# Two narrow recurrences taken chunk by chunk in turn instead of one after the other, with feed-forward blocks of 64 positions of four batches

## The chip, the cores and the metric

The kernel runs on one core of one Trainium2 chip. The metric is the device time of one execution in microseconds (us); lower is better. PE is TensorE, DVE is VectorE, ACT is ScalarE, POOL is GpSimd, SP is SyncE, which issues all DMAs here.

## The reference

Three stages follow each other. The first is a recurrence over 768 positions in 4 batches and 8 heads, with a state of 40 x 40 for each of these 32 pairs. The second and third are feed-forward layers (320 to 2048 to 320) over the 3072 tokens that the first stage gives, each with another activation.

```
for t in range(S):                                   # S = 768
    y[:, :, t] = einsum('bhd,bhde->bhe', rt, state)
    Sa = einsum('bhde,bhe->bhd', state, at)
    state = state * wt[:, :, None, :] - einsum('bhd,bhe->bhde', Sa, bt) + einsum('bhd,bhe->bhde', vt, kt)
x = y.transpose(0, 2, 1, 3).reshape(B * S, H * D)    # 3072 x 320
h = x @ w_in;   x = (h * tanh(softplus(h))) @ w_out      # layer 1 (Mish)
h = x @ w_in2;  out = (h * cos(h)) @ w_out2              # layer 2
```

The feed-forward weights arrive as 64-bit floats and are converted on the chip.

## The kernel before

**The recurrence.** Positions are taken in chunks of 32. Inside a chunk the recurrence is a small triangular system, solved by an inverse and a few matrix products; from chunk to chunk the state is handed on. A "half" (`hf`) is two of the four batches with all heads, 16 units; there are two halves of 24 chunks, 48 chunks `g` in all. Before, all chunks of half 0 come first (`hf, c = divmod(g, NCH)`), then those of half 1. So there is one chain of 48 steps.

**Work of one chunk.** `pre(g)` prepares it: a load, two scans on DVE (L548, L554), products (L562, L568), a PE group (L584) evicted in four pieces on DVE (L594), transpositions (L617). It is done up to `LA` = 8 chunks ahead. `inverse_two(bt)` inverts the triangular blocks of a batch of chunks (mostly two): out to HBM and back in another layout (L653), 28 small DVE steps (L663, L665) and a memset (L672), out and back again (L677, L681) into `TT`. `halves` finishes it chunk by chunk: a transposition on DVE (L705), PE (L700), DVE (L708), PE (L702), a copy. `chain(g)` is the serial part: PE groups L760, L773, L805, L829, L853 (two), L896 (two), with evictions on ACT and DVE between them (L765, L379, L837, L864 into `SV` for the next chunk, L872 into `Y`).

**The feed-forward layers.** They work on blocks of 256 tokens in tiles of 256 hidden features. L954 makes `h` of a tile (16 groups of matmuls), layer 1 applies Mish twice on ACT (L1026, L1028) and subtracts on DVE (L1031), so that the value goes on as a high and a low part (`GH`, `GL`); L935 multiplies with `w_out`. A block of layer 1 is four chunks: 128 positions of two batches. Layer 2 uses DVE, Sin on ACT (L1107) and POOL; its last blocks are twice as wide (L969, L985).

**The weights.** `prep` converts each layer's weights in 22 pieces of 128 x 512: a load, a copy of the upper words on ACT (L445), three integer steps on DVE (L449, L454, L459; the third puts the sign in), a rounded copy (L379 into `wih`, `wix`, `woh`) and a subtraction (L486). Layer 1's pieces are done in the first part of the kernel; layer 2's start when the recurrence is over, because they take its memory. The last five pieces of a layer go through one buffer.

**The order.** A planner (`Plan.run`) works out, from durations, hop times and priorities written in the code, in which order each engine's instructions stand. The built program keeps that order. PE is filled with feed-forward work where the recurrence has nothing ready. The planner counts a cost when PE goes from the full array to a part of it or back (`LEAVE`, `CHANGE`, `ENTER`), and time for a new activation table only where a task names its table (`aset`); the tasks of `prep` name none.

## Time and profile before

| | |
|---|---|
| runs | 1143.7 us median of 3 (1140.62 to 1145.07) |
| the profiled execution | 1147.24 us, its span 1145.5 us |
| mean granted TensorE clock | 0.983 of full speed |
| busy share | PE 91%, DVE 71%, ACT 49%, POOL 20% |

The share of an engine is a mean over three stages with different limits: the first 250 us, in which feed-forward work is scarce; the time up to about 650 us, in which recurrence and layer 1 share PE; and the rest, which is feed-forward work alone.

### The profile page before, as it was taken

What the parts mean: (1) busy time and instruction counts of PE and PEld (TensorE: products, weight loads), DVE (VectorE), ACT (ScalarE), POOL (GpSimd) and SP (SyncE); (2) the same over time, 40 slices, a digit from 0 to 9 for tenths busy, and PEclk for the clock granted to TensorE, in tenths of its full rate; (3) what the DMA queues carried; (4) which work ended last, traced back from release to release, by engine and by line L of the source; (5) the groups of instructions that cost most, each with busy time, mean ns of one, the idle gap of its engine ahead of it and who ended that gap; (6) DMA issues with size and microseconds to landing.
All of it is one profiled execution on the core that took longest, in us unless ns stands there. A gap on an engine that the chain in (4) does not pass through costs nothing.

```text
span 1145.5 us, 36557 instructions
## 1 busy us (share of the span) xinstructions
PE 1036.7 (91%) x14888; PEld 941.8 (82%) x14888; DVE 811.2 (71%) x2294; ACT 559.4 (49%) x1382; POOL 225.7 (20%) x276
## 2 busy tenths in 40 slices
PE   1345888989999899999999999999999999999998
PEld 1345677878888788888888999999999999999997
DVE  8989897868898888878973398434655555555554
ACT  3255545545656455555655476444433434343433
POOL 4124110000000000000000033111333333333333
PEclk9999989979999999989999999999999999999999
DMA  7464745445545545445443455221100101010000
GB/s 211 124 171 120 204 100 136 116 129 133 144 137 138 158 123 154 121 127 148 114 116 95 135 156 172 63 63 34 46 26 1 37 15 37 15 31 7 16 8 24
DMA packets 104183, 111.89 MB, mean 98 GB/s; under 512 B 63440, under 2 KB 84176, under 8 KB 104016
## 3 DMA queue, kind: packets, MB, share of 16 engines
q1 hardware_dynamic: 104016, 109.56, 34.6%
q8 instruction: 117, 1.92, 0.7%
q14 instruction: 50, 0.41, 0.1%
HBM read 91.43 MB, written 18.09 MB: 96 GB/s over the span
## 4 chain that ended last, share of the span: by engine, by line
PE 50%; DVE 6%; issue 2%; DMA 2%; ACT 1%; SPq 0%; POOL 0%; DVEq 0%; ACTq 0%; POOLq 0%
PE bank L969 12%; PE bank L985 11%; PE bank L954 11%; PE bank L935 11%; DMA TT<-t_d 1%; DVE SV L864 1%; PE bank L853 1%; PE bank L829 1%; PE bank L1076 1%; DVE GL L1031 1%; PE bank L805 1%; PE bank L773 1%; PE bank L760 1%; DVE FR L837 1%; DVE AM L594 1%
## 5 line engine op out<-in xcount | busy, mean ns | idle before, releaser
L1117 POOL TENSOR_TENSOR GL<-H,GH 128x512 fp32r<-128x512 f32 x96 | 123.8, 1298 | 249.6 <-ACT GH L1115 222.2
L1100 DVE TENSOR_SCALAR T<-bank 128x512 f32<-128x512 f32 x96 | 66.1, 689 | 124.1 <-PE bank L969 111.2
L379 ACT ACTIVATE FL<-bank 64x160 f32<-64x160 f32 (+1 forms) x376 | 101.7, 295 | 103.2 <-PE bank L896 54.7
L1107 ACT ACTIVATE T<-T,half_pi 128x512 f32<-128x512 f32 x96 | 69.0, 719 | 126.1 <-DVE T L1104 126.1
L1031 DVE TENSOR_TENSOR GL<-H,GH 128x512 fp32r<-128x512 f32 x96 | 68.1, 710 | 64.7 <-ACT GH L1028 64.5
L575 POOL MEMSET AM<- 64x256 f32 x96 | 29.5, 308 | 384.3 <-issue 294.3
L954 PE MATMUL bank<-XH,wih 128*128 128x256 f32 x448 | 95.4, 295 | 1.2 <-ACT GH L1028 1.1
L1026 ACT ACTIVATE H<-bank 128x512 f32<-128x512 f32 x96 | 57.3, 597 | 75.6 <-PE bank L954 73.3
L954 PE MATMUL bank<-XL,wih 128*128 128x256 f32 x448 | 90.0, 283 | 0.0
L954 PE MATMUL bank<-XH,wil 128*128 128x256 f32 x448 | 89.8, 282 | 0.0
L1115 ACT ACTIVATE GH<-H 128x512 fp32r<-128x512 f32 x96 | 60.7, 632 | 50.6 <-DVE H L1109 37.6
L853 PE MATMUL bank<-FR,FL 104*64 104x72 f32 x1536 | 67.4, 243 | 13.1 <-DVE FR L837 5.1
L1109 DVE TENSOR_TENSOR H<-bank,T 128x512 f32<-128x512 f32 x96 | 65.7, 685 | 18.0 <-ACT T L1107 17.8
L853 PEld LDWEIGHTS bank<-FR,FL 104*64 104x64 f32 x1536 | 58.8, 148 | 20.0 <-issue 8.7
L954 PEld LDWEIGHTS bank<-XH,wih 128*128 128x128 f32 x448 | 70.4, 193 | 3.2 <-ACT GH L1028 1.3
L584 PE MATMUL bank<-AM,KB 104*64 104x64 f32 x768 | 36.2, 245 | 40.3 <-DVE KB L568 18.5
L665 DVE TENSOR_TENSOR XT<-XM 64x50 f32<-64x50 f32 (+9 forms) x322 | 63.1, 197 | 10.4 <-DMA XM<-l_d 6.5
L954 PEld LDWEIGHTS bank<-XL,wih 128*128 128x128 f32 x448 | 70.0, 193 | 0.0
L954 PEld LDWEIGHTS bank<-XH,wil 128*128 128x128 f32 x448 | 69.9, 193 | 0.0
L954 PE MATMUL bank<-XH,wix 128*128 128x256 f32 x224 | 68.6, 306 | 0.0
L663 DVE TENSOR_TENSOR XM<-XM,XT 64x50 f32<-64x50 f32 (+9 forms) x322 | 64.4, 201 | 4.2 <-DVE XT L665 0.2
L1104 DVE SCALAR_TENSOR_TENSOR T<-T,bank 128x512 f32<-128x512 f32 x96 | 65.5, 682 | 1.6
(174 smaller groups left out, 2976.2 us busy)
## 6 DMA issues: line engine op xcount, KB each, us to landing
IN<-in_inT_dram SPq DMA_DIRECT2D x96, 161.4 KB
VR<-in_vR_dram SPq DMA_DIRECT2D x96, 160.0 KB
FR<-in_rI_dram SPq DMA_DIRECT2D x48, 180.0 KB
FR<-in_vF_dram SPq DMA_DIRECT2D x48, 144.0 KB
TMP<-in_w_in_dram SPq DMA_DIRECT2D x12, 512.0 KB
RA<-in_w_in_dram SPq DMA_DIRECT2D x12, 512.0 KB
RA<-in_w_out_dram SPq DMA_DIRECT2D x10, 512.0 KB
SV<-in_vS_dram SPq DMA_DIRECT2D x96, 52.0 KB
```

Of the source, the lines that this page charges most:

```text
L379: A.activation(o, i, AF.Copy)
L853: PE.matmul(fp[64 * p:64 * p + 64, qp], fl()[0:104, n * D:n * D + 64], fr()[:, n], start=True, stop=True)
L935: PE.matmul(o, l[:, f, tsl], r, start=(first and f == 0 and i == 0), stop=(last and f == 1 and i == 2))
L954: PE.matmul(hp[:, f], pss[i][0], pss[i][1], start=(i == 0), stop=(i == 7))
L969: PE.matmul(bank[P.at((key, "h"))][:, 0:512], pss[i][0], pss[i][1], start=(i == 0), stop=(i == 7))
L985: PE.matmul(o, l, r, start=(ft == 0 and i == 0), stop=(ft == NFF - 1 and i == 2))
L1031: gl = P.add(GLE, (dve(512),), lambda eng, f=f, Hv=Hv, key=key: EN[eng].tensor_tensor(out=GL_t[P.at((key, "gl"))], in0=Hv(f), in1=GH_t[P.a ...
L1100: a = P.add("DVE", dve(512), lambda f=f, hv=hv, Tv=Tv: V.tensor_scalar(out=Tv(f), in0=hv(), scalar1=0.25, scalar2=MAGIC, op0=ALU.add, op1= ...
L1104: b = P.add("DVE", dve(512), lambda f=f, hv=hv, Tv=Tv: V.scalar_tensor_tensor(out=Tv(f), in0=Tv(f), scalar=MAGIC, in1=hv(), op0=ALU.subtra ...
L1107: c = P.add("ACT", act(512, False, 1), lambda f=f, Tv=Tv: A.activation(Tv(f), Tv(f), AF.Sin, scale=-TWO_PI, bias=half_pi), preds=[b], aset ...
L1109: gt = P.add("DVE", dve(512), lambda f=f, Tv=Tv, Hv=Hv, hv=hv: V.tensor_tensor(out=Hv(f), in0=hv(), in1=Tv(f), op=ALU.mult), preds=[c, g_f ...
L1117: gl = P.add("POOL", pool(512), lambda f=f, Hv=Hv, key=key: G.tensor_tensor(out=GL_t[P.at((key, "gl"))], in0=Hv(f), in1=GH_t[P.at((key, "g ...
```

## The change

Chunk numbers now alternate between the halves (`c, hf = divmod(g, 2)`): two chains of 24 steps that need nothing of each other. The state goes to chunk `nx = g + 2`. A block of layer 1 is now 64 positions of four batches, still four chunks. Buffers of the chain (`SV`, `FR`, `VR`, `Y`) are doubled, `LA` falls from 8 to 7, every inverse batch has two chunks, one of each half, and `halves` is done once for both. The planner gets `mate`: a PE task waits a while for the same task of the other half. In `prep` the sign now comes from ACT (`AF.Prelu` with a huge negative slope in place of `AF.Copy`), and the third DVE step is gone. Buffers of the feed-forward layers are cut in halves (`H`, `T`), layer 1's last pieces of `w_out` are done in 128 x 256, and the planner's numbers are changed.

```diff
-NB = 3
+NB = 2
+NEGATIVE = -(2.0 ** 32)
-PULL, PULL_INV, PULL_CH = 0.0, 0, 0
+PULL, PULL_INV, PULL_CH = 0.3, -5000.0, -1e6
-LEAVE, CHANGE, ENTER = 0.14, 0.1, 0.09
+LEAVE, CHANGE, ENTER = 0.22, 0.12, 0.13
+WAIT = 8.0
...
+                        elif t.mate and last_mode == "full" and st - t.ready[e] < WAIT and t.mate.end is None and (
+                                t.mate.n_wait or t.mate.ready[e] > st):
+                            rank = 1.5
...
-    LA = 8
-    N_IN, N_SV, N_FR, N_X, N_VR = 2, 1, 1, 2, 1
+    LA = 7
+    N_IN, N_SV, N_FR, N_X, N_VR, N_Y, N_TT = 2, 2, 2, 2, 2, 2, 3
...
-    BATCH = [(0, 1), (1, 3)] + [(i, 2) for i in range(4, TOT, 2)]
+    BATCH = [(i, 2) for i in range(0, TOT, 2)]
...
-            t1 = P.add("ACT", act(512, False),
-                       lambda raw=raw, av=av: A.activation(av(), raw()[:, :, 1].bitcast(F32), AF.Copy, scale=REBIAS),
+            t1 = P.add("ACT", act(n, False),
+                       lambda raw=raw, av=av: A.activation(
+                           av(), raw()[:, :, 1].bitcast(F32), AF.Prelu, scale=REBIAS, alpha=NEGATIVE),
                        preds=[t0], acq=[(aring, (key, "a"))], prio=prio)
...
-            def cvt3(raw=raw, av=av, uv=uv):
-                u = uv().bitcast(U32)
-                V.scalar_tensor_tensor(out=u, in0=raw()[:, :, 1], scalar=0x80000000, in1=u,
-                                       op0=ALU.bitwise_and, op1=ALU.bitwise_or)
-
-            t3 = P.add("DVE", dve(512, 0.5), cvt1, preds=[t1], prio=prio, port=True)
-            t3 = P.add("DVE", dve(512), cvt2, preds=[t3], prio=prio, port=True)
-            t3 = P.add("DVE", dve(512), cvt3, preds=[t3], rel=[(key, "r")], prio=prio, port=True)
+            t3 = P.add("DVE", dve(n, 0.5), cvt1, preds=[t1], prio=prio, port=True)
+            t3 = P.add("DVE", dve(n), cvt2, preds=[t3], rel=[(key, "r")], prio=prio, port=True)
...
     def pre(g):
-        hf, c = divmod(g, NCH)
+        c, hf = divmod(g, 2)
...
-    def halves(bt, ci, t):
+    def halves(bt, t):
...
+    def mated(name, c, t):
+        o = mates.pop((name, c), None)
+        if o is None:
+            mates[name, c] = t
+        else:
+            o.mate, t.mate = t, o
+        return t
+
     def chain(g):
-        hf, c = divmod(g, NCH)
+        c, hf = divmod(g, 2)
+        nx = g + 2
...
-        t = P.add("PE", 0.36, rhs, preds=Gev[g] + [ldma[g], io[g][2]] + (Sev[g - 1] if c else []),
+        t = P.add("PE", 0.3, rhs, preds=Gev[g] + [ldma[g], io[g][2]] + (Sev[g - 2] if c else []),
                   acq=[("PA", k("R"))], rel=[k("AM"), k("SV")], cols=550, prio=pr)
+        mated("rhs", c, t)
...
-        if yc == 3:
-            xv = x_d[hf * 6 + yb].rearrange("(p h e) t -> p e h t", p=2, h=4)
+        if yc == 1:
+            xv = x_d[yb].rearrange("(p h e) t -> p e h t", p=2, h=4)[:, :, :, 128 * hf:128 * hf + 128]
```

The order moves at many places; three of them follow. Lines of the changed kernel have other numbers: L776 is L760 of before, L790 L773, L918 L896, L958 L935, L977 L954, L1047 and L1049 are L1026 and L1028, L1052 is L1031, L458 is L445, L389 is L379, L606 L594, L579 L568, L668 and L666 are L665 and L663, L675 L672, L710 L705, L858 L837.

**PE, the end of a chunk and the start of the next, in the part where recurrence and layer 1 share PE.** Before, the two transpositions of the new state (L896) and the first group of the next chunk (L760) stand between feed-forward rows:

```order
L617 MATMUL bank_147<-ident,KB_220 128x104 x4
L954 MATMUL bank_148<-XH_187,wih_164 128x256 x2
L954 MATMUL bank_148<-XH_187,wil_165 128x256 x2
L954 MATMUL bank_148<-XH_187,wix_166 128x256
L954 MATMUL bank_148<-XL_189,wih_164 128x256 x2
L954 MATMUL bank_148<-XL_189,wix_166 128x256
L896 MATMUL bank_144<-ident,SV_221 104x40 x4
L896 MATMUL bank_147<-ident,SV_221 104x40 x4
L760 MATMUL bank_146<-SV_221,AM_208 32x40 x16
```

Now the same groups of both halves stand together (`SV_218` and `SV_219` are the two buffers):

```order
L918 MATMUL bank_147<-ident,SV_218 104x40 x4
L918 MATMUL bank_145<-ident,SV_218 104x40 x4
L918 MATMUL bank_144<-ident,SV_219 104x40 x4
L918 MATMUL bank_146<-ident,SV_219 104x40 x4
L958 MATMUL bank_151<-woh1b,GH_180 128x320
L958 MATMUL bank_151<-wol1b,GH_180 128x320
L958 MATMUL bank_151<-woh1b,GL_182 128x320
L776 MATMUL bank_147<-SV_218,AM_203 32x40 x16
L776 MATMUL bank_145<-SV_219,AM_204 32x40 x16
```

One visit to the narrow modes serves two chunks there. Over the whole program PE's order changes its mode 531 times before and 396 times after.

**ACT, where layer 2's weights are converted while layer 1 still runs** (`AU` and `RA` are the buffers of the conversion). Before:

```order
L1026 ACTIVATE H_179<-bank_144 128x512
L1028 ACTIVATE GH_182<-bank_144 128x512
L445 ACTIVATE AU_11063<-RA_11058 128x512
L1026 ACTIVATE H_179<-bank_145 128x512
L1028 ACTIVATE GH_181<-bank_145 128x512
L445 ACTIVATE AU_11064<-RA_11059 128x512
L379 ACTIVATE wih_11045<-AU_11063 128x512
```

After:

```order
L389 ACTIVATE woh2a<-AU_11624 128x512
L458 ACT_TABLE_LOAD
L458 ACTIVATE AU_11625<-RA_11622 128x512
L1047 ACT_TABLE_LOAD
L1047 ACTIVATE H_179<-bank_144 128x512
L1049 ACTIVATE GH_180<-bank_144 128x512
L458 ACT_TABLE_LOAD
L458 ACTIVATE AU_11623<-RA_11620 128x512
L1047 ACT_TABLE_LOAD
```

Loads of activation tables stand between the two kinds of work. The whole program had 3 of them and has 34: one at the start, one at the first Mish, 8 more in the conversion of layer 1's last pieces, 23 in that of layer 2 with 16 tiles of layer 1 among them, and one for Sin. Before, 4.6 blocks of layer 1 are left when the recurrence ends; after, 2.3.

**DVE, an inverse and the transposition of its result.** Between the memset that ends the inverse and the transposition lie two DMAs. Before, in the thirteenth batch:

```order
L672 MEMSET XM_225 64x16
L562 TENSOR_TENSOR AM_206<-IN_192,PE_198 40x256
L568 TENSOR_TENSOR KB_220<-IN_192,RP_218 104x8x32
L381 COPY FR_222<-bank_144 32x4x40
L837 TENSOR_TENSOR FR_222<-bank_146,maskR 64x4x2x32
L1031 TENSOR_TENSOR GL_183<-H_179,GH_181 128x512
L837 TENSOR_TENSOR FR_222<-bank_146,maskR 64x4x2x32
L594 TENSOR_TENSOR AM_206<-bank_145,maskG 64x4x32 x2
```

The transposition (L705) of that batch comes six rows later. After, in the seventeenth batch:

```order
L666 TENSOR_TENSOR XM<-XM,XT 64x14
L675 MEMSET XM 64x16
L606 TENSOR_TENSOR AM_201<-bank_144,maskG 64x4x32 x4
L579 TENSOR_TENSOR KB_217<-IN_193,RP_215 104x8x32 x2
L710 STREAM_TRANSPOSE TA<-TT_232 128x256
L606 TENSOR_TENSOR AM_202<-bank_145,maskG 64x4x32 x2
L858 TENSOR_TENSOR FR_220<-bank_146,maskR 64x4x2x32
```

Only six instructions stand between the two there.

## Rows read from the trace of the kernel before

**Rows 1.** Busy time by stage: from:to, length, engines, then PEclk, DMA share, GB/s:

```profile
0.00:100.00 100.00, 38.95 (x896) 32.30 (x896) 92.57 (x291) 40.24 (x105) 30.83 (x69) 1.00 0.60 168
100.00:250.00 150.00, 123.47 (x2529) 107.96 (x2533) 127.51 (x427) 77.63 (x225) 23.25 (x35) 0.93 0.51 136
250.00:650.00 400.00, 385.20 (x8323) 341.04 (x8314) 316.31 (x1146) 220.16 (x666) 16.51 (x54) 0.98 0.48 128
650.00:725.00 75.00, 73.59 (x571) 72.60 (x566) 55.20 (x75) 46.97 (x84) 24.74 (x17) 1.00 0.47 151
850.00:1120.00 270.00, 270.00 (x1513) 244.60 (x1512) 151.08 (x244) 108.67 (x184) 94.33 (x74) 1.00 0.06 19
```

**Rows 2.** Groups on DVE: count, busy us, mean ns of one, idle before:

```profile
L459 DVE SCALAR_TENSOR_TENSOR H<-TMP,H 128x512 uint32<-128x512 uint32 x8 | 5.4, 679 | 0.0
L548 DVE TENSOR_TENSOR_SCAN PE<-IN,D 104x264 f32<-104x264 f32 x48 | 34.5, 718 | 0.3 <-DMA IN<-in_inT_dram 0.3
L562 DVE TENSOR_TENSOR AM<-IN,PE 40x256 f32<-40x256 f32 x96 | 40.8, 425 | 1.3
L594 DVE TENSOR_TENSOR AM<-bank,maskG 64x128 f32<-64x128 f32 x192 | 55.0, 286 | 6.5 <-PE bank L584 2.1
L665 DVE TENSOR_TENSOR XT<-XM 64x50 f32<-64x50 f32 (+9 forms) x322 | 63.1, 197 | 10.4 <-DMA XM<-l_d 6.5
L663 DVE TENSOR_TENSOR XM<-XM,XT 64x50 f32<-64x50 f32 (+9 forms) x322 | 64.4, 201 | 4.2 <-DVE XT L665 0.2
```

**Rows 3.** Timeline of DVE, start and length, around the 12th chunk's end:

```profile
231.16 0.28 DVE L872 TENSOR_TENSOR Y<-bank,PE 104x128 f32<-104x128 f32 x1
```

**Rows 4.** Timeline of PE where narrow groups stand among layer 1's rows:

```profile
307.89 0.31 PE L935 MATMUL bank<-woh1a,GL 128*128 128x320 f32 x1
308.12 0.41 PE L896 MATMUL bank<-ident,SV 40*104 40x40 f32 x8
308.89 0.42 PE L935 MATMUL bank<-woh1a,GH 128*128 128x320 f32 x1
309.15 0.31 PE L935 MATMUL bank<-wol1a,GH 128*128 128x320 f32 x1
```

**Rows 5.** Groups on ACT, 650 to 790 us:

```profile
L1026 ACT ACTIVATE H<-bank 128x512 f32<-128x512 f32 x37 | 22.1, 598 | 43.9 <-PE bank L954 43.9
L445 ACT ACTIVATE AU<-RA 128x512 f32<-128x512 f32 x22 | 14.6, 673 | 1.3 <-DMA RA<-in_w_out_dram 1.2
```

**Rows 6.** Timeline of ACT around a table load, and two neighbours later on:

```profile
135.76 0.63 ACT L379 ACTIVATE woh1b<-H 128x512 fp32r<-128x512 f32 x1 [2.67 <-DVE H L459]
136.41 1.28 ACT L1026 ACT_TABLE_LOAD   x1
137.70 0.60 ACT L1026 ACTIVATE H<-bank 128x512 f32<-128x512 f32 x1
...
783.21 0.60 ACT L1026 ACTIVATE H<-bank 128x512 f32<-128x512 f32 x1 [0.73 <-PE bank L954]
783.70 0.59 ACT L1028 ACTIVATE GH<-bank 128x512 fp32r<-128x512 f32 x1
```

**Rows 7.** The chain that ended last, two tiles of layer 1:

```profile
654.78 3.65 PE bank L954 x32
658.43 3.51 PE bank L935 x24
```

**Rows 8.** The same chain at an inverse's DMAs; then a PE group:

```profile
465.45 3.35 DMA t_d<-XM
468.85 4.54 DMA TT<-t_d
...
L700 PE MATMUL bank<-TA,TT 16*32 16x32 f32 x1536 | 23.7, 202 | 17.3 <-DVE TA L705 13.4 <-DVE XT L665 2.6 <-DVE AM L594 1.0
```

**Rows 9.** Timeline, a weight load's issue and the ACT instruction that waits for it:

```profile
730.72 0.35 SPq L440 DMA_DIRECT2D RA<-in_w_out_dram  x1
...
734.53 0.66 ACT L445 ACTIVATE AU<-RA 128x512 f32<-128x512 f32 x1 [0.79 <-DMA RA<-in_w_out_dram]
```

295 lines of the change are left out of this document (154 added, 141 removed).

## The prediction

> **What bounds the kernel now.** I read the stages first [rows 1]. In the first 100 us PE is busy for 39 us and DVE for 92.6; from 100 to 250 us PE idles another 26.5 us while DVE is busy for 127.5 of 150. So DVE sets the pace until feed-forward work is plentiful. From 250 to 650 us PE is busy for 385 of 400 us, and from 650 us on it hardly stops (270 of 270 from 850 to 1120). From then on the end is wherever PE's work ends: what moves the time is PE time lost at the start, PE time spent on changing modes, and any stall put into the later part. Next, what a row costs: DVE's forms [rows 2], the place where the 12th chunk's `Y` leaves DVE [rows 3], a change of mode on PE [rows 4], ACT's forms [rows 5], a table load among its neighbours [rows 6], a feed-forward tile on PE [rows 7], the DMAs around an inverse [rows 8] and a weight load [rows 9].
>
> **The start: -27 us, of which 6 come back.** I summed DVE's rows in program order, each at the duration of its form, up to the last `Y` of the 12th chunk: 224.5 us before, 198.2 after. The trace reaches that place at 231.16 + 0.28 = 231.4 us [rows 3], 1.03 times the sum, so DVE's row sum is a fair clock there. The 26.3 us are: 22 steps of L459 at 0.68, 15.0; two chunks and one inverse fewer done ahead (per chunk two scans of 0.72, two products of 0.425 and two of another form costed alike, four evictions of 0.29, so 4.3; an inverse is 63.1 + 64.4 us over 23 batches, 5.5), 14.1 [rows 2]; 1.6 for joint transpositions; less 4.4 for more set-up and smaller pieces. PE's rows up to that place, at full-clock costs, come to the same in both orders (120.6 and 120.3 us, feed-forward part included), so the 27 us (26.3 x 1.03) are a gain and no work pushed back. Bounds: nothing, if something else than DVE becomes late; 33, if DVE's idle time in the first 250 us shrinks as well.
>
> Against this stand 8 new table loads on ACT among the first two blocks of layer 1. Each takes 1.28 us, and from the end of the instruction before it to the start of the next one 137.70 - 136.39 = 1.31 us passed, where two neighbours otherwise overlap by 0.11 [rows 6]: 1.4 us each, 11 us. ACT is busy 52% in that stretch [rows 1], but RS, ZS, FR, VR and FL of the chain queue behind each load. I charge half, 6 us (bounds 0 and 11).
>
> **Recurrence and layer 1 together: -11 us.** PE's rows change mode 531 times before and 396 after, 103 of the 135 fewer behind the 12th chunk. In the trace the last L935 before a narrow group takes 308.12 - 307.89 = 0.23 us and the first one after it 309.15 - 308.89 = 0.26 [rows 4], where 24 in a row take 3.51 us, 0.146 each [rows 7]: about 0.08 to 0.11 a change, 0.11 taken, 11 us. That the joint groups halve the visits is thus true at few places only; a quarter is what the order shows. The matmuls themselves are the same in number. Does PE stay the bound? From the 12th chunk to the last, PE's rows, each at its form's duration, sum to 408 us before and DVE's to 375, where the trace took some 419 (to about 650 us); after, PE's to 459 (2.2 more blocks of layer 1 stand among them) and DVE's to 398. PE leads by more than before. Bounds: 0, where chain waits fill the freed time; 15 with the granted clock at full, which was 0.98 in this stage [rows 1], 8 us of lost clock at most; as much again is lost if joint narrow groups pull it down.
>
> **Layer 2's weights: +17 us.** Here the change costs. After, 23 table loads stand among the last 16 tiles of layer 1. On PE a tile is 32 matmuls of L954 and 24 of L935, 3.65 + 3.51 us for two of them [rows 7], so 16 tiles take 57.3. On ACT the same stretch holds 32 Mish of 0.60 (19.2), 18 `AU` steps of 0.67 (12.1), 21 copies of 0.63 (13.2) [rows 5, 6], nine short evictions (3.7, an estimate at two thirds of a Mish), 48.2 together, 43.7 with the overlap of some 45 neighbours, a tenth each [rows 6]. That is under 57.3, and PE was indeed busy for 73.6 of 75 us there [rows 1]. With 23 loads at 1.31, 30.1, it is 73.8: ACT becomes the bound and PE waits for `GH` for 16.5 us; 17 taken. Lower bound 8, if PE runs two or three tiles ahead where loads are dense and catches up on the two tiles at the end that have none; upper bound 30, if ACT, an in-order queue, also waits for DVE's converted pieces and for PE's transpositions with loads still to come. L459 gone here saves nothing, as DVE is busy 55 of 75 us and PE does not wait for it; without that cover its 22 steps would count, 15 us at the 0.68 of [rows 2].
>
> [...]
>
> **The last five pieces: +4 us.** They go through one `RA2`: load, `AU`, two DVE steps, the next load. From issue to use 734.53 - 730.72 = 3.8 us pass [rows 9], with `AU`'s 0.67 [rows 5] and two DVE steps of at most L459's 0.68 behind them up to 5.8 us a piece. Before, 4.6 blocks of layer 1 were left to hide all of it; after, block 0 of layer 2 needs piece 3 to 5 in tiles 5 to 7, at (3.65 + 3.51) / 2 = 3.58 us a tile [rows 7]. Two us lost for each of the last two pieces; bounds 0 and 10.
>
> **Costed at nothing.** Halved `H` and `T`: a tile's life (three DVE steps, Sin, a copy, a POOL step) is shorter than the three tiles of 3.6 us that the ring lasts, and PE's full 270 us [rows 1] cover it. More and smaller output DMAs: DMA is at 6% there. Doubled `FR`, `VR`, `SV`: loads are earlier, none was waited for long. Lookahead 7 for 8: PE is the bound, and a rival holds what remains.
>
> **Sum.** -27 + 6 - 11 + 17 + 4 = -11 on the profiled execution's 1147.2 us (span 1145.5): 1136. That execution is 3.5 us above the median of 1143.7, so the same difference gives 1133 there. I take 1134.
>
> **Rivals.**
> Loads hidden: PE's lead of two to three tiles (four `h` buffers after the recurrence) and ACT's idle half absorb them. For it: ACT waited 44 us for PE's `h` in this part [rows 5]. Against it: the sum of rows, 73.8 over 57.3. Of the 27 us that give back, 6 stay: 1134 - 21 = 1113.
>
> Late transpositions, which ends slower: the result of an inverse needs two DMAs, 3.35 and 4.54 us [rows 8], after its last step, and its transposition stands in DVE's in-order queue. Before, DVE had 5 to 10 us of rows between the two in nearly all batches, and waits there still cost PE 13.4 us (the idle time before L700 that ended on `TA`) [rows 8]. After, five of 24 batches have under 3.5 us between (the DVE order shown is such a place: four evictions of 0.29 and two products of at most 0.425, 2.0 us [rows 2]), and now both chains wait behind it, and Mish's DVE step too. If DVE gets there early, 5 batches x 5.5 us = 27 us, less what feed-forward rows on PE cover, 23 taken: 1157. It decides once DVE reaches the transposition more than some 3 us ahead of the landing; DVE's slack (398 of 459 us) makes that likely, PE's filled order makes it cheap.
>
> The start gains nothing: not DVE but the chain through ACT or the DMAs (0.60 of the time busy in the first 100 us [rows 1]) sets the pace once DVE has 26 us less. Then 21 us are missing: 1155.
>
> [...]
>
> **Chances.** My forecast 0.45 (1122 to 1146 with its own bounds), loads hidden 0.19 (1104 to 1122), late transpositions 0.22 (1146 to 1170), no gain at the start 0.09, drain 0.05. Half a per cent, about what a measurement here can tell from no change, is 5.7 us: faster is under 1138, slower over 1149.4. Faster: 0.29 of the first, all of the second, 0.02 of the others, 0.50. Slower: 0.18, 0.07, 0.05 less a little, 0.27. Same: 0.23. The range leaves a tenth out on each side: 1110 to 1160.
>
> **What would show it.** Right: the 12th chunk's `Y` at about 210 us (231 before); the recurrence over at about 675 to 690; in the stretch with `AU` some 23 loads of 1.28 us, ACT busy over 90%, PE 75 to 80%, waits of L935 for `GL` behind `GH`; full PE after it. Wrong: PE full there, or waits of over 2 us before each transposition in DVE's queue, or a 12th chunk at 225 us or later, or a granted clock under 0.95 between 250 and 650 us.

## The result and the profile after

The changed kernel takes 1154.4 us (median of 4, 1152.61 to 1155.64), the kernel before 1142.2 beside it (1139.37 to 1145.07): 1.0106 times as long, 95% interval 1.0074 to 1.0137. It is slower, where about 1134 and faster was forecast. The profiled executions differ by less, 1153.0 us of span for 1145.5, since that of before took 3.5 us more than the median of its first three runs; the accounts below compare these two.

From the page of the changed kernel, its busy time:

```profile
PE 1025.2 (89%) x14888; PEld 935.7 (81%) x14888; DVE 805.2 (70%) x2212; ACT 599.3 (52%) x1403; POOL 221.5 (19%) x278
```

Its windows by stage, with the columns of [rows 1]:

```profile
0.00:100.00 100.00, 36.23 (x816) 30.15 (x816) 87.97 (x253) 39.43 (x98) 30.70 (x67) 1.00 0.62 172
100.00:250.00 150.00, 131.22 (x2747) 117.14 (x2740) 130.15 (x422) 92.28 (x252) 20.79 (x40) 0.98 0.50 136
250.00:650.00 400.00, 376.77 (x7685) 343.82 (x7685) 317.71 (x1072) 213.41 (x619) 16.31 (x54) 0.98 0.46 120
711.00:795.00 84.00, 70.20 (x483) 65.35 (x482) 36.59 (x61) 74.39 (x105) 24.49 (x18) 0.96 0.38 119
850.00:1120.00 270.00, 270.00 (x1522) 244.63 (x1521) 154.07 (x244) 111.09 (x189) 94.42 (x73) 1.00 0.09 22
```

To 250 us PE is busy for 5 us more than before and DVE for 2 less, from 250 to 650 PE is busy for 8 us less, and the last row is full as before. The row that had none like it is 711 to 795: PE 70.2 of 84 us, ACT 74.4. There layer 2's weights are converted beside the last tiles of layer 1.

DVE's timeline gives two ends, the 12th chunk's last `Y` ([rows 3] has it before) and the last `Y` of all:

```profile
224.59 0.29 DVE L893 TENSOR_TENSOR Y<-bank,PE 104x128 f32<-104x128 f32 x1
...
699.92 0.29 DVE L893 TENSOR_TENSOR Y<-bank,PE 104x128 f32<-104x128 f32 x1 [0.21 <-PE bank L874]
```

The 12th chunk is done at 224.9 us, 6.6 earlier and not the 21 to 27 of the forecast. The recurrence ends at 700, as against about 650, with more of layer 1 already done.

An account closes over both spans. For each stage I took PE's matmuls by form, each at the spacing that its form has at full clock where nothing waits (0.114 us for L954 and 0.146 for L935 by [rows 7], the others in the same way), and what is left of the stage is lost: idle time, mode changes, a lower clock. Stages end at the 12th chunk's last narrow group on PE, at the last narrow group of all, and at the last group of L954 (L977 after), which is also used by layer 2's first blocks.

| lost on PE, us | start | middle | layer 1's rest, conversion | layer 2 | after PE's last | sum |
|---|---|---|---|---|---|---|
| before | 128.2 | 72.3 | 4.8 | 1.5 | 4.7 | 211.5 |
| after | 117.6 | 67.0 | 24.9 | 2.1 | 7.5 | 219.1 |
| difference | -10.6 | -5.3 | +20.1 | +0.6 | +2.8 | +7.6 |
| forecast | -21 | -11 | +21 | 0 | 0 | -11 |

So the dear term was forecast and came; two gains came at half their size, and a small loss at the end had been costed at nothing. The account holds for the two profiled executions; by the medians the distance is 12.2 us.

ACT's groups from 700 to 800 us answer to [rows 5]:

```profile
L458 ACT ACT_TABLE_LOAD x12 | 15.4, 1283 | 0.2
L1047 ACT ACT_TABLE_LOAD x11 | 14.1, 1283 | 0.2
L458 ACT ACTIVATE AU<-RA 128x512 f32<-128x512 f32 x19 | 12.3, 670 | 0.1
L1047 ACT ACTIVATE H<-bank 128x512 f32<-128x512 f32 x18 | 10.8, 598 | 11.1 <-PE bank L977 10.9
```

ACT's timeline there, start and length, answers to [rows 6]:

```profile
731.47 1.28 ACT L458 ACT_TABLE_LOAD   x1
732.76 0.68 ACT L458 ACTIVATE AU<-RA 128x512 f32<-128x512 f32 x1
733.46 1.28 ACT L1047 ACT_TABLE_LOAD   x1
734.75 0.60 ACT L1047 ACTIVATE H<-bank 128x512 f32<-128x512 f32 x1
735.25 0.59 ACT L1049 ACTIVATE GH<-bank 128x512 fp32r<-128x512 f32 x1
```

And PE's waits from 700 to 800 us (us in total, times, longest) name what PE stood for:

```profile
PE bank L958 <- ACT GH L1049: 12.0, 8, 2.5
PE bank L958 <- DVE GL L1052: 1.5, 9, 0.2
```

23 loads of 1.28 us, 29.5 us in all, more than either kind of work they serve. The next instruction starts 0.01 us after a load (732.76 after 731.47 + 1.28), so a pair of loads costs ACT the 2.6 us that it takes and, besides, only the 0.1 us by which two neighbours otherwise overlap (735.25 for 734.75 + 0.60). In these rows of the timeline ACT does not stand still; from 711 to 795 it is idle for 9.6 of 84 us, and PE waits 12.0 us for `GH`.

### The profile page after: what moved, and what is told of

Read it like the earlier page. It is cut to its first block, busy times and chain, and to the rows that moved or that the text cites. A ratio compares the mean times of both kernels' runs of the same rounds, so it can differ in the third digit from the quotient of the medians.

```text
span 1153.0 us, 36365 instructions
## 1 busy us (share of the span) xinstructions
PE 1025.2 (89%) x14888; PEld 935.7 (81%) x14888; DVE 805.2 (70%) x2212; ACT 599.3 (52%) x1403; POOL 221.5 (19%) x278
## 4 chain that ended last, share of the span: by engine, by line
PE 53%; DVE 14%; ACT 7%; issue 5%; DMA 3%; SPq 2%; POOL 0%; DVEq 0%; ACTq 0%; POOLq 0%
PE bank L992 12%; PE bank L1008 11%; PE bank L958 11%; PE bank L977 9%; DVE SV L885 2%; DVE FR L858 1%; DVE AM L606 1%; DVE XM L666 1%; DVE XT L668 1%; ACT L1047 1%; ACT L458 1%; PE bank L874 1%; PE bank L596 1%; DVE Y L893 1%; DVE GL L1052 1%
## 5 line engine op out<-in xcount | busy, mean ns | idle before, releaser
L389 ACT ACTIVATE FL<-bank 40x160 f32<-40x160 f32 (+1 forms) x375 | 101.2, 295 | 117.4 <-PE bank L629 60.0
L1052 DVE TENSOR_TENSOR GL<-H,GH 128x512 fp32r<-128x512 f32 x96 | 66.8, 696 | 64.6 <-ACT GH L1049 63.7
L977 PE MATMUL bank<-XH,wih 128*128 128x256 f32 x448 | 95.0, 294 | 0.8 <-ACT GH L1049 0.8
L1047 ACT ACTIVATE H<-bank 128x512 f32<-128x512 f32 x96 | 57.4, 598 | 68.1 <-PE bank L977 67.1
L977 PE MATMUL bank<-XL,wih 128*128 128x256 f32 x448 | 89.7, 282 | 0.0
L977 PE MATMUL bank<-XH,wil 128*128 128x256 f32 x448 | 89.2, 281 | 0.0
L668 DVE TENSOR_TENSOR XT<-XM 64x26 f32<-64x26 f32 (+6 forms) x336 | 67.9, 202 | 16.2 <-DMA XM<-l_d 8.1
L874 PE MATMUL bank<-FR,FL 104*64 104x72 f32 x1536 | 64.4, 241 | 12.9 <-issue 6.1
L666 DVE TENSOR_TENSOR XM<-XM,XT 64x26 f32<-64x26 f32 (+6 forms) x336 | 68.9, 205 | 8.2
L596 PEld LDWEIGHTS bank<-AM,KB 104*64 104x64 f32 x768 | 31.0, 157 | 52.7 <-issue 44.2
L977 PEld LDWEIGHTS bank<-XH,wih 128*128 128x128 f32 x448 | 69.9, 191 | 3.2 <-ACT GH L1049 1.3
L958 PE MATMUL bank<-woh1a,GH 128*128 128x320 f32 x192 | 65.3, 340 | 7.9 <-ACT GH L1049 7.8
L606 DVE TENSOR_TENSOR AM<-bank,maskG 64x128 f32<-64x128 f32 x192 | 55.1, 287 | 24.7 <-PE bank L596 18.6
L977 PEld LDWEIGHTS bank<-XL,wih 128*128 128x128 f32 x448 | 69.6, 192 | 0.0
```

What stands on the lines that cost most here:

```text
L389: A.activation(o, i, AF.Copy)
L596: PE.matmul(gp[c0:c0 + 64, q // 2], kb()[:, q].rearrange("p a t -> p (a t)"), am()[0:104, :, q], start=True, stop=True)
L666: V.tensor_tensor(out=b[:, 0:i, i + 1:16], in0=b[:, 0:i, i + 1:16], in1=tv, op=ALU.add)
L668: V.tensor_tensor(out=tv, in0=bc(b[:, i:i + 1, i + 1:16], (2 * n, i, w)), in1=bc(b[:, 0:i, i:i + 1], (2 * n, i, w)), op=ALU.mult)
L874: PE.matmul(fp[64 * p:64 * p + 64, qp], fl()[0:104, n * D:n * D + 64], fr()[:, n], start=True, stop=True)
L958: PE.matmul(o, l[:, f, tsl], r, start=(first and f == 0 and i == 0), stop=(last and f == 1 and i == 2))
```

## The experiments

Where nothing else is said, an edit is to the changed kernel. Ratios are to the kernel before, on the same chip, and "lost" is the account above, by stage. The diffs are shortened to the lines that matter; the `lambda` heads around the calls are left out.

### Price of the table loads

Copy instead of Prelu for all pieces, then for layer 2's alone. The instructions stand in the order of the changed kernel, and only the table loads are gone.

```diff
-    av(), raw()[:, :, 1].bitcast(F32), AF.Prelu, scale=REBIAS, alpha=NEGATIVE),
+    av(), raw()[:, :, 1].bitcast(F32), AF.Copy, scale=REBIAS),
```

> The changed kernel with Copy in place of Prelu in the conversion of both layers' weights, every instruction in the same order; the sign of the weights is left out. ACT's table loads fall from 34 to 3. Theory (the loads are what PE pays for): where layer 2's weights are converted PE idled 13.8 us in the changed kernel, 12.0 of them waiting for GH; at most 3 of that stays, and the clock loss beside it goes too, 13 to 18 us; at the start DVE's 4.9 us of waits for ACT's converted pieces go, worth 2 to 5 us at the end. 1154 becomes 1132 to 1139. Rival (PE really waits for the conversion's single last buffer, the loads are hidden): at most 5 us, 1149 or more.

> The same in layer 2's weights alone (their sign is left out), same order: 23 loads fewer, the 8 early ones stay. Theory: 13 to 18 us, so 1136 to 1141, and 2 to 5 us slower than with all of them gone. Rival (the early loads are the dear ones, since they stand in the recurrence's serial chain): under 8 us here, 1146 or more.

Measured: 1127.2 us, ratio 0.989 (0.9833 to 0.9947), with all loads gone; 1132.5, 0.9919 (0.9888 to 0.995), with layer 2's gone. That is 22 us for the 23 loads by medians and 21 by the ratios, above the theory's 13 to 18, and some 5 for the 8 early ones, though there the two intervals overlap. The window of the stretch in the second kernel reads:

```profile
711.00:795.00 84.00, 83.06 (x643) 82.29 (x642) 54.45 (x82) 55.21 (x100) 34.34 (x26) 1.00 0.45 142
```

PE is busy for 83.1 of 84 us for 70.2, and its only wait from 700 to 800 us is one of 0.9 for `GL`; the clock is 1.00 for 0.96, ACT is busy for 55.2 us for 74.4. The loss there is 3.9 us for 24.9, and the other stages stay within 2.0. The 21 us of that stretch are thus the loads' price, shown by taking them away alone. Nothing is left for the last five pieces, whose single buffer is as it was.

### Versions that keep the sign

Prelu only in the 17 pieces that come before the first Mish; in the others Copy again, with the third DVE step behind the second and every other instruction in its place.

```diff
-    av(), raw()[:, :, 1].bitcast(F32), AF.Prelu, scale=REBIAS, alpha=NEGATIVE),
+    av(), raw()[:, :, 1].bitcast(F32), AF.Prelu, scale=REBIAS, alpha=NEGATIVE)) if layer == 1 and not late else
+    av(), raw()[:, :, 1].bitcast(F32), AF.Copy, scale=REBIAS)),
...
+    if sign:
+        V.scalar_tensor_tensor(out=u, in0=raw()[:, :, 1], scalar=0x80000000, in1=u,
+                               op0=ALU.bitwise_and, op1=ALU.bitwise_or)
```

> The changed kernel with Prelu only in the 17 pieces of layer 1 that are converted before the first Mish; the other pieces of both layers take Copy again and the third DVE step for the sign, put into the task of the second step, so every other instruction stays in its order. Table loads 34 to 3. Theory: as fast as with Copy everywhere and no sign (1127), plus at most 4 for the third step in layer 2's conversion and in the last pieces of layer 1: 1127 to 1133, faster than before. Rival (that run was fast because DVE lacked work there; with the third step back PE waits for the conversion): 1137 or more.

Measured: 1152.8 us, ratio 1.0121 (1.0075 to 1.0168): the rival. The loss at the conversion is 20.1 us, without one table load there. PE's waits from 690 to 850 us:

```profile
PE bank L963 <- DVE GL L1057: 5.6, 7, 2.0
PE bank L963 <- ACT GH L1054: 2.9, 2, 1.7
```

DVE's timeline at one of them:

```profile
759.15 0.68 DVE L470 SCALAR_TENSOR_TENSOR AU<-RA,AU 128x512 uint32<-128x512 uint32 x1
759.86 0.69 DVE L473 SCALAR_TENSOR_TENSOR AU<-RA,AU 128x512 uint32<-128x512 uint32 x1
760.47 0.68 DVE L470 SCALAR_TENSOR_TENSOR AU<-RA,AU 128x512 uint32<-128x512 uint32 x1
761.19 0.69 DVE L473 SCALAR_TENSOR_TENSOR AU<-RA,AU 128x512 uint32<-128x512 uint32 x1
761.80 1.75 DVE L1057 TENSOR_TENSOR GL<-H,GH 128x512 fp32r<-128x512 f32 x1
```

Layer 1's subtraction (L1057 here), for which PE stands, is behind four conversion steps in DVE's queue, of which two (L473) are the added ones, and takes 1.75 us itself. (It started 0.5 us into a piece of 1.70 us that POOL subtracts. Where L1057 starts during such a piece, it ends 0.55 us after the piece does, in seven of eight cases of this run; otherwise it takes about 0.7.) I had forecast that L459 "gone here saves nothing, as DVE is busy 55 of 75 us". In this order it does save something: where loads cost 21 us, the steps they replaced cost 16.

Another version lets the planner know the added step, a task of its own:

```diff
+t3 = P.add("DVE", dve(n), cvt3, preds=[t3], rel=[(key, "r")], prio=prio, port=True)
```

> The changed kernel with Prelu in the 17 early pieces of layer 1 alone, Copy and a third DVE step in the others, the step now a task that the planner knows, so the order is made anew (407 mode changes for 395). Theory (in the run with the unplanned third step PE lost 20 us at layer 2's conversion because layer 1's subtraction stood behind conversion steps in DVE's queue, by an order that did not count them): the loss there falls to 5 to 10, the time to 1136 to 1144. Rival (2.3 blocks of layer 1 are too little cover for the conversion in any order with three DVE steps): 15 us or more lost there, 1148 or more.

Measured: 1162.9 us, ratio 1.0189 (1.0152 to 1.0227), and 21.6 us lost at the conversion: the rival again. An order that counts the step loses as much, so the order that left it out was not to blame. The kernel before did the same three steps for 4.8 us; it had 4.6 blocks of layer 1 left beside them, here about 2. That this cover makes the difference is argued: no run varied it alone.

And the planner told of the table, with a penalty for changing it:

```diff
+PRE = ("prelu",)
-key = (max(st - t.pull if e == "DVE" else st, f + SLACK[e]), rank, t.prio + (5e4 if sw else 0), order[id(t)])
+key = (max(st - t.pull if e == "DVE" else st + 5 * sw, f + SLACK[e]), rank, t.prio + (5e4 if sw else 0), order[id(t)])
-preds=[t0], acq=[(aring, (key, "a"))], prio=prio)
+preds=[t0], acq=[(aring, (key, "a"))], aset=PRE, prio=prio)
```

> The changed kernel with Prelu as it is, but the planner is told its table and puts a task that needs another table back by five loads' time, so that conversions and Mish stand in groups: 17 table loads for 34, 12 for 23 at layer 2's conversion; the order is made anew (406 mode changes for 395). Theory (the price goes by the number of loads, 0.9 us each): the loss at layer 2's conversion falls from 25 to about 15, the early part gains 2, 1141 to 1146. Rival (the price is that conversion and Mish share ACT in so short a stretch; grouping makes each wait longer for the other): the loss stays at 20 or more, 1150 or more.

Measured: 1158.7 us, ratio 1.0156 (1.0115 to 1.0197). The conversion lost 19.2 us, between the two; the new order lost 9.6 more at the start, so the time itself says little. PE's longest waits there show what became of the price:

```profile
PE bank L978 <- ACT GH L1050: 9.1, 2, 7.6
```

Two waits, one of 7.6 us, in place of eight of up to 2.5. Half the loads took away a quarter of the loss.

### The old order with Prelu

The kernel before, with Prelu and without the third step in both layers, planned anew:

```diff
-A.activation(av(), raw()[:, :, 1].bitcast(F32), AF.Copy, scale=REBIAS)
+A.activation(av(), raw()[:, :, 1].bitcast(F32), AF.Prelu, scale=REBIAS, alpha=NEGATIVE)
-t3 = P.add("DVE", dve(512), cvt3, preds=[t3], rel=[(key, "r")], prio=prio, port=True)
```

> The kernel before with Prelu and no third DVE step in both layers, planned anew: 36 table loads more, all but one of them among the layer-1 tiles at which layer 2's weights are converted, of which 4.6 blocks are left there. Theory (loads cost only where layer 1's PE work is too short to cover ACT: here 37 tiles of 3.58 us, 132, against some 78 us of ACT before and 47 of loads): 3 to 10 us lost there, 9 to 13 gained at the start, 1132 to 1142. Rival (each load costs PE 0.9 us as in the changed kernel, 21 us for 23, whatever the cover): 1160 or more.

Measured: 1143.9 us, ratio 1.0026 (0.9993 to 1.0058). Start and middle gained 9.4 and 10.3 us, and the conversion lost 26.7, 21.9 more than before: above the theory, below the 33 that the rival's 0.9 us would make of 36 loads. The windows of this kernel:

```profile
650.00:700.00 50.00, 41.79 (x280) 38.64 (x280) 24.85 (x37) 48.83 (x66) 16.30 (x12) 0.93 0.47 152
700.00:790.00 90.00, 85.26 (x636) 83.39 (x635) 28.91 (x46) 59.92 (x93) 12.06 (x9) 0.98 0.18 54
```

Over the whole stretch ACT has room, as I had reckoned, but not in its first 50 us: there it is busy for 48.8 and PE for 41.8. Cover is counted where the loads stand and not over the stage.

### Where the start's gain went

Copy and the third step in the 17 early pieces too, on top of the kernel that has Prelu in these alone:

```diff
-    av(), raw()[:, :, 1].bitcast(F32), AF.Prelu, scale=REBIAS, alpha=NEGATIVE)) if layer == 1 and not late else
+    av(), raw()[:, :, 1].bitcast(F32), AF.Prelu, scale=REBIAS, alpha=NEGATIVE)) if False else
```

> As the run before it, but the 17 early pieces too take Copy and the third DVE step: 17 steps of 0.6 us net, 10 us of DVE time, return to the first 100 us. Theory (DVE sets the pace at the start, so its time there comes out at the end): 7 to 11 us slower than with Prelu in these pieces, the 12th chunk's Y 8 to 11 later. Rival (the start is paced by something else, and this is why the prediction's 27 us came as 11): under 4 us.

Measured: 1164.4 us, ratio 1.0204 (1.0169 to 1.0239), 11.7 us more than the run that it is compared with, in the same series; the 12th chunk's `Y` comes at 236.6 for 225.8, 10.8 later for 13.6 of durations. Most of the DVE time added to the start comes out at the end.

The planner's pull set to 0:

```diff
-PULL, PULL_INV, PULL_CH = 0.3, -5000.0, -1e6
+PULL, PULL_INV, PULL_CH = 0.0, 0, 0
```

> The changed kernel with the planner's pull set to 0 as before, so that the steps of an inverse no longer go ahead of other DVE work; the order moves at many places. Theory: in the changed kernel neighbours on DVE overlap by 15 us less up to the 12th chunk because dependent steps stand side by side; without the pull they are interleaved again, that overlap returns by 8 to 15 us, the 12th chunk's Y comes at 212 to 218 us (224.9 with it), and the time falls by 5 to 10: 1144 to 1149. Rival (the overlap went with the pairing of batches, not with the pull): the 12th chunk within 3 us of 225, the time within 5 us of 1154.

Measured: 1159.4 us, ratio 1.015 (1.0117 to 1.0183). The theory fell. Up to the 12th chunk the pairs of inverse steps that stand next to each other fell from 88 to 43, as many as before the change, but the overlap came to 17.1 us for 15.1. That chunk's `Y` came at 219.3, between the two expectations, and the kernel was slower even so.

The kernel before with one inverse in work at a time:

```diff
-N_IN, N_SV, N_FR, N_X, N_VR = 2, 1, 1, 2, 1
+N_IN, N_SV, N_FR, N_X, N_VR = 2, 1, 1, 1, 1
```

> The kernel before with one buffer for inverses instead of two, so that the dependent steps of two inverses can't stand between one another on DVE; the order is made anew. Theory (neighbours on DVE overlap only where they don't depend on each other, and with the pairing of chunks one inverse at a time is in work, which took 15 us of overlap at the start): the overlap up to the 12th chunk's Y falls from 30 to under 22 us there, the Y comes 6 us or more later than 231, the time rises to 1148 or more. Rival (the overlap was lost with the order of other work, not with the second inverse): overlap above 26, the Y within 3 us of 231, the time within 4 of before.

Measured: 1134.7 us, ratio 0.9943 (0.9904 to 0.9981), overlap 27.1 us for 30.3, the 12th chunk's `Y` at 233.8 for 231.4. The theory fell here too: the second inverse does not make the overlap. The overlap and the `Y` are the rival's; the time fell by some 5 to 7 us, a little more than its 4, and the order is new.

Then I counted the overlaps inverse by inverse. In the changed kernel the neighbours of the odd-numbered inverses (first, third and so on) overlap in 244 of 337 places, those of the even-numbered in 70 of 353. Every second inverse lies in the upper half of `XM`, a part of the change that the forecast did not look at:

```diff
-    XL_m = [at.tile([128, 544], F32, name=f"XM{i}") for i in range(N_X)]
+    XM = at.tile([128, 544], F32, name="XM")
...
+        rows = lambda: slice(64 * P.at(("X", bt)), 64 * P.at(("X", bt)) + 2 * n)
```

Both buffers began at partition 0 before; now the second begins at 64. Two kernels put it to the test, with one buffer, at 0 and at 64, and one order for both:

```diff
-    N_IN, N_SV, N_FR, N_X, N_VR, N_Y, N_TT = 2, 2, 2, 2, 2, 2, 3
+    N_IN, N_SV, N_FR, N_X, N_VR, N_Y, N_TT = 2, 2, 2, 1, 2, 2, 3
```

and in the second of them also

```diff
-        rows = lambda: slice(64 * P.at(("X", bt)), 64 * P.at(("X", bt)) + 2 * n)
+        rows = lambda: slice(64, 64 + 2 * n)
```

> The changed kernel with one buffer for inverses, always in partitions 0 to 63 (before the change both buffers began at partition 0; the change put the second at partition 64); the order is made anew. In the changed kernel's trace, the neighbours of the first, third, fifth inverse overlap in about three of four places, those of the second, fourth, sixth in one of five. Theory (work at partition 64 between work at partition 0 is what takes the overlap): neighbours of every inverse overlap in three of four places, the overlap to the 12th chunk's Y is 22 us or more for 15, the Y comes 8 us or more before that of the run with partitions 64 to 127, and the time is 8 to 20 us shorter than that run's. Rival (the place in partitions is nothing to DVE, every second inverse merely stands among other work): both runs within 3 us, the same share of overlaps in both.

> The same kernel and, instruction for instruction, the same order, with the one buffer in partitions 64 to 127. Theory: the neighbours of every inverse overlap in one of five places, the overlap to the 12th chunk's Y is under 14 us, the Y 8 us or more later than in the run with partitions 0 to 63, and the time 8 to 20 us longer. Rival: within 3 us of that run.

Measured: 1133.9 us at partition 0, ratio 0.9942 (0.9917 to 0.9967), and 1187.9 at 64, ratio 1.041 (1.0362 to 1.0459). 54 us lie between them, over twice the theory's upper end, for the place of a buffer. Of the 756 neighbours of inverse steps 564 overlap at 0 and 133 at 64. DVE's timeline shows the same stretch in both, three rows from its start and three from its end (start, length), first at 0:

```profile
146.78 0.15 DVE L668 TENSOR_TENSOR XT<-XM 64x26 f32<-64x26 f32 x1
146.86 0.41 DVE L468 SCALAR_TENSOR_TENSOR RL<-RL 128x256 uint32<-128x256 uint32 x1
147.19 0.17 DVE L666 TENSOR_TENSOR XM<-XM,XT 64x26 f32<-64x26 f32 x1
...
148.23 0.41 DVE L573 TENSOR_TENSOR AM<-IN,PE 40x256 f32<-40x256 f32 x1
148.57 0.18 DVE L666 TENSOR_TENSOR XM<-XM,XT 64x36 f32<-64x36 f32 x1
148.67 0.41 DVE L579 TENSOR_TENSOR KB<-IN,RP 104x256 f32<-104x256 f32 x1
```

And at 64:

```profile
156.71 0.18 DVE L668 TENSOR_TENSOR XT<-XM 64x26 f32<-64x26 f32 x1
156.92 0.43 DVE L468 SCALAR_TENSOR_TENSOR RL<-RL 128x256 uint32<-128x256 uint32 x1
157.38 0.18 DVE L666 TENSOR_TENSOR XM<-XM,XT 64x26 f32<-64x26 f32 x1
...
158.77 0.42 DVE L573 TENSOR_TENSOR AM<-IN,PE 40x256 f32<-40x256 f32 x1
159.22 0.19 DVE L666 TENSOR_TENSOR XM<-XM,XT 64x36 f32<-64x36 f32 x1
159.44 0.42 DVE L579 TENSOR_TENSOR KB<-IN,RP 104x256 f32<-104x256 f32 x1
```

At partition 0 a neighbour starts before the one ahead of it has ended (146.86 for 146.78 + 0.15); at 64 it starts some 0.03 after that end (156.92 for 156.71 + 0.18). From the first to the last start 1.89 us pass at 0 and 2.73 at 64. That the place alone does this is shown, 564 overlaps for 133 in one order; what on DVE makes the neighbour wait is not.

What is lost on PE shows where it hurts:

| lost on PE, us | start | middle | layer 1's rest, conversion | layer 2 | after PE's last | sum |
|---|---|---|---|---|---|---|
| at partition 0 | 117.8 | 45.7 | 27.1 | 1.6 | 7.6 | 199.8 |
| at partition 64 | 135.0 | 81.0 | 26.4 | 1.6 | 7.5 | 251.5 |

17 us at the start, 35 in the middle. Against the changed kernel the one buffer at 0 gains 21.3 us in the middle and nothing at the start (117.8 for 117.6). In the middle PE waits for `GL`, which stands behind inverse steps and other rows in DVE's queue; the waits (us in total, times, longest) read at 0:

```profile
PE bank L958 <- DVE GL L1052: 2.6, 8, 0.6
```

And at 64:

```profile
PE bank L958 <- DVE GL L1052: 19.9, 16, 2.1
```

### Faster versions

The kernel before, its old order kept, with Prelu for layer 1's pieces and their third step left empty:

```diff
-    A.activation(av(), raw()[:, :, 1].bitcast(F32), AF.Copy, scale=REBIAS),
+    (A.activation(av(), raw()[:, :, 1].bitcast(F32), AF.Prelu, scale=REBIAS, alpha=NEGATIVE)) if layer == 1 else
+    (A.activation(av(), raw()[:, :, 1].bitcast(F32), AF.Copy, scale=REBIAS)),
...
+                if layer == 1:
+                    return
```

> The kernel before, with the sign of layer 1's weights taken by Prelu and the third DVE step of these 22 pieces left empty; every other instruction stays in its order. ACT gets 4 table loads more. Theory (at the start DVE's time comes out at the end, and neighbours' overlap takes nothing of it here since no order is moved): 22 steps of 0.60 us net, 13, less up to 4 for the loads: 9 to 13 us faster than before, 1130 to 1135. Rival (most of it is taken back by other waits, as in the changed kernel): under 6 us, 1138 or more.

Measured: 1133.6 us, ratio 0.9943 (0.9912 to 0.9973). That is 8.8 us by medians and 6.5 by the ratio, between the two expectations; in the trace DVE's durations to the 12th chunk shrink by 14.9 us, its waits grow by 6.7 and neighbours overlap by 2.9 less, so that chunk comes 5.3 earlier.

The kernel before with one inverse in work, in that run's order, and the same edit:

```diff
-N_IN, N_SV, N_FR, N_X, N_VR = 2, 1, 1, 2, 1
+N_IN, N_SV, N_FR, N_X, N_VR = 2, 1, 1, 1, 1
```

> The kernel before with one buffer for inverses, in the order of the run before this one, and the sign of layer 1's weights by Prelu with the third DVE step left empty; no table load is added. Theory (DVE time taken out of the start comes out at the end wherever DVE is the engine that works without a pause there): 7 to 12 us faster than the run before, the 12th chunk's Y at 211 to 216 for 222, 0.982 to 0.988 of the kernel before. Rival (what is taken from DVE comes back as its waits once it is 9 us faster, as two thirds did in the changed kernel): under 4 us, the Y at 219 or later, 0.991 or more.

Measured: 1128.5 us, ratio 0.9872 (0.9833 to 0.991). Against the run without Prelu that is some 8 us by the two ratios, 6 by medians, about the theory's lower end, with intervals that just overlap. The `Y` moves by 3.8 us only, nearer the rival: from 233.8 to 230.0, since the 222 of the expectation is the 11th chunk's. Durations are 15.2 less, waits 8.2 more, overlap 3.2 less.

The changed kernel with one buffer at partition 0 and Prelu in the 17 early pieces alone:

```diff
-    N_IN, N_SV, N_FR, N_X, N_VR, N_Y, N_TT = 2, 2, 2, 2, 2, 2, 3
+    N_IN, N_SV, N_FR, N_X, N_VR, N_Y, N_TT = 2, 2, 2, 1, 2, 2, 3
-    av(), raw()[:, :, 1].bitcast(F32), AF.Prelu, scale=REBIAS, alpha=NEGATIVE),
+    av(), raw()[:, :, 1].bitcast(F32), AF.Prelu, scale=REBIAS, alpha=NEGATIVE)) if layer == 1 and not late else
+    av(), raw()[:, :, 1].bitcast(F32), AF.Copy, scale=REBIAS)),
```

> The changed kernel with one buffer for inverses in partitions 0 to 63, in that run's order, and Prelu only in the 17 pieces before the first Mish; the others take Copy and a third DVE step behind the second. Three table loads are left of 30. Theory (in the order with the inverses at partition 64 the loads' absence and the third step cancelled but for a few us; DVE now has more room, so the third step costs less): 4 to 10 us faster than with the loads, 1124 to 1130, 0.985 to 0.991 of the kernel before. Rival (the third step costs at the conversion what the loads cost, whatever DVE saves elsewhere): within 3 us of 1134.

Measured: 1128.7 us, ratio 0.988 (0.9848 to 0.9912), 5.2 below the same kernel with the loads; 20.1 us are lost at the conversion for 27.1. The theory holds. With the run ahead of it, from the old order, it is the fastest here that takes the sign along; which of the two is faster can't be told.

### The pairing, and the stores

No waiting for the mate:

```diff
-WAIT = 8.0
+WAIT = 0.0
```

> The changed kernel in which a PE task no longer waits for the same task of the other half; PE's order changes its mode 484 times instead of 395. Theory (a change costs about 0.12 us of PE where PE is the bound): 8 to 11 us slower than the changed kernel, 1162 to 1166. Rival (what fewer changes give is taken by waits, since both chains must meet): within 3 us of 1154.

Measured: 1174.4 us, ratio 1.0292 (1.0249 to 1.0335), 20 us slower than the changed kernel, twice the theory: 10 us more lost at the start, 7.5 in the middle. Taken by the account of the middle, 65 changes more cost 6.0 us besides waits, 0.09 each; the rest is waits, the more so at the start. In these two orders the pairing pays.

One output DMA for a tile instead of two:

```diff
-for i in range(2):
-    r0 = (2 * jj + i) * S + 64 * b1
-    SP.dma_start(out[r0:r0 + 64], OB_t[P.at(ok)][64 * i:64 * i + 64])
+o = out.rearrange("(b s) d -> b s d", b=4)[2 * jj:2 * jj + 2, 64 * b1:64 * b1 + 64]
+SP.dma_start(o, OB_t[P.at(ok)])
```

> The changed kernel with one output DMA for each tile of 128 rows instead of two of 64 rows, nothing else moved. Theory: the last block's eight issues on SP, 5.66 us, become four in about 3.2, and the span ends 2.4 us earlier: 1152. Rival (the time behind the last matmul is the DMA's own, which carries the same rows): no change, 1154.

Measured: 1180.1 us, ratio 1.0375 (1.0303 to 1.0447), worse than either expected. It doesn't test the end, since the DMA itself became slow, 8.41 us for 2.15; the last section has its rows. The 5.66 us in this expectation and the next is no time of issuing, as the account of the end below shows.

The second of each tile's DMAs on ACT's queue in the last blocks, on top of Prelu in the 17 early pieces:

```diff
+q = A if i and b1 >= 10 else SP
+q.dma_start(out[r0:r0 + 64], OB_t[P.at(ok)][64 * i:64 * i + 64])
```

> As the first of these three, and in the last blocks the second of each tile's two output DMAs is issued on ACT's queue. Theory (the 5.66 us in which SP issues the last eight DMAs end the span): 2 to 3 us faster than the first. Rival (a DMA's own time ends it): under 0.5 us.

Measured: 1150.1 us, ratio 1.0081 (1.0053 to 1.0109), 2.6 below its partner by medians, with intervals that overlap. In the profiles the time behind PE's last matmul falls from 7.4 to 6.5 us only. Not settled by the times; in the trace 0.9 of the 2 to 3 us is seen.

## Why the prediction was wrong

**Layer 2's weights: right in mechanism, a little small.** 17 us for 23 loads was forecast; they cost 21. "The last five pieces: +4 us" was wrong, they cost nothing that can be seen (3.9 us lost in the whole stretch without loads, 4.8 before). Together 21 were forecast and 20.1 came, which is luck: one term was too small and the other too large. "L459 gone here saves nothing" was wrong as well, but it entered no sum; the likely reason, argued and not shown, is the cover that the change took away, from 4.6 blocks of layer 1 to 2.3.

**The start: the step that failed.** "So DVE's row sum is a fair clock there": the sum fell as reckoned, from 236.1 us of DVE durations to 210.0 in the traces, 26.1 for my 26.3. But durations plus waits, less the overlap of neighbours, make the time: 236.1 + 25.6 - 30.3 = 231.4 before, 210.0 + 30.0 - 15.1 = 224.9 after. That the 1.03 of before came out so near to one was the waits and the overlap nearly in balance. The change halved the overlap, because it laid every second inverse at partition 64: the two runs that differ in that alone have 22.0 and 9.6 us of overlap up to the 12th chunk and lie 54 us apart with all 24 inverses there or none, and the changed kernel has 12, some 27 by that, an estimate. With one buffer at partition 0 the changed kernel takes 1133.9 us, in an order made anew, 20 less. That this equals the forecast of 1134 is luck: the start gave half of what was forecast there too, the middle over twice as much.

What the place cost at the start of the changed kernel itself is not shown. With one buffer at 0 the overlap there is 6.9 us larger, but the waits are 9.6 larger too, and the 12th chunk's `Y` comes at 226.4 for 224.9. Two buffers that both begin at 0, as before the change, were not run.

The waits at the start grew as well. The largest in DVE's list up to 225 us that before lacks is this:

```profile
DVE RL L463 <- ACT RL L458: 4.9, 6, 2.1
```

Pieces came late from ACT, but hardly because of its table loads: without any load the same row still has 3.2 us. Why is open. The 6 us charged for the early loads were about right: some 5 us of time by medians lie between the runs with and without them.

The row sum has another limit. DVE time added to the start was paid for the most part (10.8 us at the 12th chunk for 13.6 of durations), DVE time taken away gave a quarter to a third there (3.8 and 5.3 of 15), the rest turning into waits and lost overlap. So even at partition 0 the start gained 10.4 us and not 21, and the middle 26.6, of which the new order has a share that I did not part from the buffer's.

**Recurrence and layer 1 together: right in mechanism, half eaten.** 103 changes fewer were to give 11 us. What PE lost there besides idle time fell from 53.7 to 40.7, a little more than that, 2 or 3 us of it the clock (0.98 granted from 225 to 700 us for 0.97 from 231 to 650; an estimate). But its idle time rose from 18.6 to 26.2. PE's longest wait in this stage of the changed kernel:

```profile
PE bank L958 <- DVE GL L1052: 6.8, 5, 2.5
```

The same row of the kernel before:

```profile
PE bank L935 <- DVE GL L1031: 0.9, 2, 0.7
```

New is the wait for `GL`, 6.8 us for 0.9; it is 2.6 with the inverses at partition 0 and 19.9 with them at 64. "PE leads by more than before" was true of the sums of rows, and these did not know what the rows would cost after the change.

**The end: costed at nothing.** "More and smaller output DMAs: DMA is at 6% there." SP's last issues stand in one row of its timeline, in the changed kernel:

```profile
1144.72 5.66 SPq L1154 DMA_DIRECT2D out_dram<-OB  x8
```

And before:

```profile
1140.02 3.18 SPq L1132 DMA_DIRECT2D out_dram<-OB  x4
```

I first took these lengths for the time of issuing, and two expectations rest on that. They hold pauses: one issue takes 0.47 to 0.60 us after and 0.33 to 0.37 before, so 4.3 of the 5.66 us and 1.4 of the 3.18 are issuing. SP pauses because there are two output buffers, and ACT fills one again only when its DMA has landed. ACT's timeline shows the waits, in the changed kernel:

```profile
1147.47 0.44 ACT L1146 ACTIVATE OB<-bank 128x320 f32<-128x320 f32 x1 [2.33 <-DMA out_dram<-OB]
1148.81 0.44 ACT L1146 ACTIVATE OB<-bank 128x320 f32<-128x320 f32 x1 [0.91 <-DMA out_dram<-OB]
```

And before:

```profile
1141.93 0.91 ACT L1128 ACTIVATE OB<-bank 128x320 f32<-128x320 f32 x2 [1.50 <-DMA out_dram<-OB]
```

3.2 us of waiting for 1.5: 1.7 of the 2.8 us by which the span's end lies later behind PE's last matmul. The rest lies behind the last of these instructions, where two issues of 64 rows follow instead of one of 128. With the issues on two queues ACT still waits 2.6 us, which fits the small gain of that run. No other work hides the last DMAs, so a mean share was the wrong row to read.

**The rivals.** Late transpositions gave 1157 and no gain at the start 1155, the nearest figures. The first was not what happened: DVE's waits for the inverse's DMA shrank, as a row of its waits shows, of the changed kernel:

```profile
DVE TA L710 <- DMA TT<-t_d: 7.2, 4, 3.1
```

And of the kernel before:

```profile
DVE TA L705 <- DMA TT<-t_d: 10.2, 8, 3.6
```

"Loads hidden" is refuted by the run without them. "The start gains nothing" was half true, and for a reason that it did not name. The drain to which the forecast gives a chance of 0.05, time lost beside a load, no run shows: the rows above have a load of 1.28 us, 0.02 us after the end of the instruction ahead of it (733.46 after 732.76 + 0.68), and the next instruction 0.01 us after the load.

**What the forecast named as signs.** About 23 loads in the stretch with `AU`: 23. ACT over 90% busy and PE 75 to 80%: 89 and 84 in the window from 711 to 795. The recurrence over at 675 to 690: 700. A 12th chunk at 225 us or later was to show it wrong: 224.9.

## What to carry to other kernels

Look where in the partitions a buffer begins, not only how large it is: moving the inverses from partition 0 to 64, a line that looks like housekeeping, cost 54 us with all of them moved and the order kept (some 27 for every second one, an estimate), and it shows in the timeline as neighbours on DVE that no longer overlap (133 of 756 do, for 564); so a sum of durations is a clock only while waits and overlaps stay as they were. Another function on ACT can put a table load at each change of work: with Prelu in place of Copy the trace has 34 of them for 3, 1.28 us each. Count the loads in the order of the built program and weigh them against ACT's busy time in the tens of us where they stand, since 23 of them cost PE 0.9 us each with ACT at 52% over the span. Work that is done earlier may no longer cover what it used to cover: with 2.3 blocks of layer 1 less at the end of the recurrence, conversion steps that had been hidden cost 16 us, though no run varied the cover alone. Open a merged row of a timeline before reading its length as work: the last eight issues span 5.66 us and take 4.3.
